# Second token group prepared in block 7, weight sums in two halves, and a block sum kept in SBUF

## The chip, the cores and the metric

The kernel runs on one core of one Trainium2 chip. TensorE (PE) does the matrix products, VectorE (DVE), ScalarE (ACT) and GpSimd (POOL) the element-wise work, and SyncE (SP) issues nearly all transfers; each of the five works through its own queue in order. The metric is the time of one execution in microseconds, as the median of several runs.

## The reference

Three networks follow each other. Attention over 4 x 8 heads of 576 positions, each query seeing up to 32 keys (dense for half of the heads, every fourth for the others); then a gated network; then eight experts, all of which see all 2304 tokens, weighted by a matrix P that is balanced in eight rounds.

```python
attn = softmax(masked(q @ k.T / 8)) @ v            # 2304 tokens x 512
x  = attn / rms(attn) * rms_g
x  = (silu(x @ w_gate) * (x @ w_val)) @ w_out      # 512 -> 1536 -> 512
P  = balance(exp(x @ w_gate2))                     # 2304 x 8
out = sum(P[:, e:e+1] * (relu(x @ w1[e]) @ w2[e])  # 512 -> 1024 -> 512
          for e in range(8))
```

## The kernel before

*Numbers in two parts.* Each operand of a product is split into a high part (a cast, ACT) and a low part (a subtraction, POOL or DVE), and three products high x high, high x low, low x high make one. So every operand costs a cast and a "low half".

*First network.* The tokens lie in eight blocks of 256 and 320. For each slice f of 128 hidden columns, `gemm_h` makes the gate (pg) and the value (pv); ACT's SiLU writes hf (L473), DVE multiplies (L474), ACT casts h (L475), POOL makes its low half (L476). Every four slices `gemm_out` adds up po, with ACT (L444) or DVE (L446) taking it out of PSUM into `partial`, which goes to x2d in DRAM (L448). Beside block i runs the attention of block i+1 (`att_tile`): the ssq of a tile gives its power on POOL (L292, an instruction of 128x2), DVE scales xs by it (L294), TensorE transposes it (L300). Beside it also run the `gate` of the experts, which fetches x2d slice by slice (sx, L582), casts it (g, L590) and makes its low half on POOL (L591), and `weight_sums`.

*Weight sums.* The second network multiplies blocks by a scheme with seven products (`STEPS`) in place of eight; for this it needs sums of weight blocks. `weight_sums` makes these for 16 chunks of both weights: 64 items, each loaded into one of three buffers (the unused parts of kbd and vbd, and conv), summed by four operations on POOL or DVE, and stored into `sums`. The four operations are ordered behind the newest hf product and h low half (`marks["late"]`).

*Token pieces.* The tokens are in three groups of 768. The sums and high and low parts of the first group's tokens are made at the end of block 7 (`tail`: `x_load`, `x_split`). Those of the other two are made by `x_prepare` during the second network, one group ahead: six pieces, each with four loads of 128x128 from x2d (xr), four subtractions on DVE, one cast on ACT (xh, L546) and one low half on DVE (xl, L549), and two stores to `xparts`. They take three tiles of the pool wx, from which the weights of the second network come too.

*Second network.* 48 units, 16 chunks for each of three groups. `gemm1(u)` makes seven products of 12 matmuls, `gemm2(u-1)` seven of 18, in turns. In the last step of `gemm1` the ReLU and four sums (`relu_with`, L998) give s1 to s4, which `summed` casts (L993) and halves (L994): s1 on DVE from PSUM, the others on POOL. In the first group the second weights are split from raw (L685, L686), and afterwards read back from DRAM.

*Order.* The functions above are generators, and `spread` advances them beside the matmuls' steps, so many steps of each to a block: 24 of `weight_sums`. A scheduler that simulates a timeline then sets the order of each queue from that; on the chip every queue runs in the order set.

## Time and profile before

| | us |
|---|---|
| median of three runs | 2108.41 (2107.94 to 2114.29) |
| profiled execution | 2112.69 |
| its span, first to last instruction | 2110.9 |
| TensorE busy in the span | 2023.5 |
| VectorE, ScalarE, GpSimd busy | 1440.8, 1097.3, 1167.6 |

In the rows of windows the busy times stand in the order PE, PEld (weight loads), DVE, ACT, POOL, then the granted clock, the busy share of the DMA engines and GB/s.

Attention and the first network fill the span up to about 640 us; the second network follows, its first group to about 1170 us. The granted clock in the windows is a share of TensorE's full 2.4 GHz: 0.50 is its lower level of 1.2 GHz. Idle time of an engine other than TensorE costs nothing by itself; it matters where TensorE waits behind it.

### The profile page before, as it was taken

The page shows a single profiled execution, that of the slowest core. Times are in us where ns is not written, and L with a number is a line of the kernel's source. Part 1 is how long each engine was busy: PE and PEld are TensorE (multiplying, and loading weights), DVE is VectorE, ACT ScalarE, POOL GpSimd, SP SyncE. Part 2 cuts the span into 40 slices and gives each one's busy share as a digit, 9 for nine tenths or more (in the row PEclk, how much of TensorE's full clock was granted, in tenths as well). Part 3 has the DMA queues.
Part 4 walks back from the last instruction along what each step waited for, and adds up shares of the span by engine and source line. Part 5 has one row for each costly group of instructions (what it writes and reads, how often), then busy time and mean ns, then how long its engine had stood idle before and what let it go on. Part 6 is the DMA issues. An engine that isn't in the chain of part 4 may idle for free.

```text
span 2110.9 us, 42653 instructions
## 1 busy us (share of the span) xinstructions
PE 2023.5 (96%) x16102; PEld 1976.6 (94%) x16102; DVE 1440.8 (68%) x3006; ACT 1097.3 (52%) x2408; POOL 1167.6 (55%) x1132
## 2 busy tenths in 40 slices
PE   5789999999998998999999999999999999999999
PEld 4688899899898998999999999999999999999999
DVE  7986544444435989888887676677766666667666
ACT  6564433333246575665656645555555645555553
POOL 3675555555555556766766545554554545544452
PEclk7899999999999999999999999999999999999999
DMA  8423676666647767788789756666668665566652
GB/s 269 146 74 104 236 254 223 239 234 213 215 138 267 253 218 257 267 287 293 255 284 362 250 190 199 230 230 222 215 214 293 235 200 183 187 210 200 198 178 85
DMA packets 210015, 464.69 MB, mean 220 GB/s; under 512 B 17168, under 2 KB 59920, under 8 KB 209808
## 3 DMA queue, kind: packets, MB, share of 16 engines
q1 hardware_dynamic: 202752, 442.97, 61.5%
q10 hardware_dynamic: 7056, 18.98, 2.8%
q8 instruction: 127, 2.08, 0.4%
q14 instruction: 80, 0.66, 0.1%
HBM read 349.16 MB, written 112.72 MB: 219 GB/s over the span
## 4 chain that ended last, share of the span: by engine, by line
PE 73%; DVE 9%; DMA 7%; POOL 4%; ACT 3%; issue 3%; SPq 1%; ACTq 0%; DVEq 0%; POOLq 0%
PE ya L1067 17%; PE pa L1014 16%; PE yb L1067 8%; PE pb L1014 8%; PE pv L461 5%; PE pg L461 5%; PE yc L1067 4%; PE po L435 4%; PE pc L1014 4%; DMA w0r<-in_w 2%; DMA sx<-x2d 1%; DMA sums<-vbd 1%; DMA w0s<-sums 1%; POOL w_s L686 1%; DVE h_a L986 1%
## 5 line engine op out<-in xcount | busy, mean ns | idle before, releaser
L686 POOL TENSOR_TENSOR w_s<-w0s,w_s 128x512 fp32r<-128x512 f32 x192 | 260.3, 1360 | 94.6 <-ACT w_s L685 94.5
L994 POOL TENSOR_TENSOR h_s<-p,h_s 128x384 fp32r<-128x384 f32 x96 | 103.4, 1098 | 354.7 <-ACT h_s L993 306.4
L686 POOL TENSOR_TENSOR w_a<-w0r,w_a 128x512 fp32r<-128x512 f32 x144 | 195.7, 1360 | 154.0 <-ACT w_a L685 153.4
L1103 DVE SCALAR_TENSOR_TENSOR acc<-ya,Pm,acc 128x256 f32<-128x256 f32 x510 | 220.9, 474 | 66.0 <-PE ya L1067 65.7
L1067 PE MATMUL ya<-w_t,h_s 128*128 128x256 f32 x1728 | 228.0, 283 | 1.6 <-ACT acc L1092 0.8
L1014 PE MATMUL pa<-x_t,w_s 128*128 128x384 f32 x1152 | 226.5, 338 | 2.5 <-ACT p L1026 2.5
L1067 PEld LDWEIGHTS ya<-w_t,h_s 128*128 128x128 f32 x1728 | 220.6, 190 | 2.6 <-ACT acc L1092 1.1
L1014 PEld LDWEIGHTS pa<-x_t,w_s 128*128 128x128 f32 x1152 | 199.9, 190 | 2.9 <-ACT p L1026 2.9
L461 PE MATMUL pv<-xn,w_v 128*128 128x320 f32 (+1 forms) x1152 | 185.6, 304 | 12.9 <-DVE w_v L380 3.6
L461 PE MATMUL pg<-xn,w_g 128*128 128x320 f32 (+1 forms) x1152 | 183.8, 303 | 3.9 <-DVE hf L474 2.5
L461 PEld LDWEIGHTS pv<-xn,w_v 128*128 128x128 f32 x1152 | 164.8, 193 | 18.9 <-DVE w_v L380 4.8
L435 PE MATMUL po<-h,w_o 128*128 128x320 f32 (+1 forms) x1152 | 175.6, 300 | 6.4 <-POOL w_o L378 1.6
L685 ACT CAST w_s<-w0s 128x512 fp32r<-128x512 f32 x192 | 120.2, 626 | 109.2 <-PE pb L1014 64.8
L1103 DVE SCALAR_TENSOR_TENSOR acc<-yb,Pm,acc 128x256 f32<-128x256 f32 x258 | 109.4, 475 | 93.0 <-PE yb L1067 92.8
L461 PEld LDWEIGHTS pg<-xn,w_g 128*128 128x128 f32 x1152 | 164.6, 193 | 8.1 <-DVE hf L474 3.3
L435 PEld LDWEIGHTS po<-h,w_o 128*128 128x128 f32 x1152 | 159.8, 189 | 11.0 <-DVE partial L446 2.6
L476 POOL TENSOR_TENSOR h<-hf,h 128x256 fp32r<-128x256 f32 (+1 forms) x96 | 82.2, 859 | 110.4 <-ACT h L475 110.1
L994 POOL TENSOR_TENSOR h_s<-r,h_s 128x384 fp32r<-128x384 f32 x96 | 98.9, 1053 | 53.0 <-ACT h_s L993 48.6
L1067 PE MATMUL yc<-w_b,h_a 128*128 128x256 f32 x864 | 124.1, 286 | 3.4 <-DVE acc L1096 1.6
L685 ACT CAST w_a<-w0r 128x512 fp32r<-128x512 f32 x144 | 89.5, 623 | 70.5 <-DMA w0r<-in_w 21.8
L1067 PE MATMUL yb<-w_t,h_s 128*128 128x256 f32 x864 | 121.8, 283 | 1.6 <-ACT h_s L993 1.0
L1067 PE MATMUL yb<-w_t,h_a 128*128 128x256 f32 x864 | 121.0, 282 | 1.8 <-DVE acc L1103 1.1
(258 smaller groups left out, 4749.0 us busy)
## 6 DMA issues: line engine op xcount, KB each, us to landing
w_t<-split SPq DMA_DIRECT2D x128, 512.0 KB, 4.3
w0r<-in_w SPq DMA_DIRECT2D x96, 512.0 KB, 6.4
w0s<-sums SPq DMA_DIRECT2D x96, 512.0 KB, 7.4
w_b<-split SPq DMA_DIRECT2D x96, 512.0 KB, 3.7
split<-w_t SPq DMA_DIRECT2D x64, 512.0 KB, 3.2
split<-w_b SPq DMA_DIRECT2D x48, 512.0 KB, 3.8
w1r<-in_w SPq DMA_DIRECT2D x32, 512.0 KB, 5.6
w1s<-sums SPq DMA_DIRECT2D x32, 512.0 KB, 7.6
```

Source lines behind the costliest of these rows:

```text
L435: nc.tensor.matmul(po[:, :n], lhsT=ow[f][:, a, dc * P : dc * P + P], rhs=hs[blk, f][:, bb, :n], start=k == 0, stop=k == 11,)
L461: nc.tensor.matmul(ps[:, :n], lhsT=w[kt, fg][:, a, fo * P : fo * P + P], rhs=xn[:, kt, bb, :n], start=k == 0, stop=k == 11,)
L476: late_g = nc.gpsimd.tensor_tensor(out=h[:, 1, :n], in0=hf, in1=h[:, 0, :n].bitcast(F32), op=ALU.subtract)
L685: nc.scalar.copy(v[:, :, 0, :], src)
L686: lo_eng.tensor_tensor(out=v[:, :, 1, :], in0=src, in1=v[:, :, 0, :].bitcast(F32), op=ALU.subtract)
L986: nc.vector.scalar_tensor_tensor(out=h[:, 1, :], in0=src, scalar=0.0, in1=h[:, 0, :].bitcast(F32), op0=ALU.max, op1=ALU.subtract)
L994: eng.tensor_tensor(out=h[:, 1, :], in0=src, in1=h[:, 0, :].bitcast(F32), op=ALU.subtract)
L1014: nc.tensor.matmul(ps, lhsT=w1s[u, a][:, kt, hl, q * P : q * P + P], rhs=xc[b, kt][:, xl, :TH], start=fresh and k == 0, stop=k == 5, skip_ ...
L1067: nc.tensor.matmul(ps, lhsT=hh[u, a, q][:, hl, jj * P : jj * P + P], rhs=w2s[u, b][:, q, wl, :], start=fresh and k == 0 and jj != 1, stop= ...
L1103: nc.vector.scalar_tensor_tensor(out=dst, in0=ps, scalar=scale, in1=dst, op0=ALU.mult, op1=ALU.add)
```

## The change

Three edits. The pieces of the second group (g = 1) are no longer made in the second network, but behind the weight sums, in the same three buffers (`ahead`); the third group's still are, by `x_prepare(2)` beside the second group. The four operations of a weight sum are given in two parts of two, each behind the newest marks, and `weight_sums` has three steps an item where it had two; `spread` now gets 39 steps a block. In `gemm1` the sum s1 is written over its operand u4 in SBUF and no longer over the PSUM bank; all low halves of s1 to s4 are on POOL, and they are made in the order s2, then s4 and s3, then s1.

```diff
+    def x_piece(g, k, c, raw, place):
+        b11, t3, t2, b21, t1, t4, b22 = (raw[:, P * j : P * j + P] for j in range(7))
+        for dst, i, j in ((b11, 0, 0), (t3, 0, 1), (b21, 1, 0), (b22, 1, 1)):
+            c0 = GT * g + TH * j + P * c
+            nc.sync.dma_start(dst, x2d[k + 2 * i, :, c0 : c0 + P])
+        yield
+        nc.vector.tensor_tensor(out=t1, in0=t3, in1=b11, op=ALU.subtract)
+        nc.vector.tensor_tensor(out=t3, in0=b22, in1=t3, op=ALU.subtract)
+        nc.vector.tensor_tensor(out=t2, in0=b22, in1=t1, op=ALU.subtract)
+        nc.vector.tensor_tensor(out=t4, in0=b21, in1=t2, op=ALU.subtract)
+        hi = place()
+        nc.scalar.copy(hi, raw)
+        yield
+        lo = raw.bitcast(F32R)
+        nc.vector.tensor_tensor(out=lo, in0=raw, in1=hi.bitcast(F32), op=ALU.subtract)
+        for n, t in enumerate((hi, lo)):
+            nc.sync.dma_start(
+                xparts[g - 1][:, k, :, n, P * c : P * c + P].rearrange("m p n -> p m n"),
+                t.bitcast(F32).rearrange("p (m n) -> p m n", m=7),
+            )
...
-            late.close()
-            nc.sync.dma_start(sums[w, ch][:, k, :], t.rearrange("p i n -> p (i n)"))
-            yield
-            load(i + 2)
-            yield
+            for part in range(2):
+                with ExitStack() as late:
+                    for m in marks["late"]:
+                        late.enter_context(tc.issue_after(m.ins))
+                    for out_, in0, in1, op in ops[2 * part : 2 * part + 2]:
+                        eng.tensor_tensor(out=out_, in0=in0, in1=in1, op=op)
+                if part:
+                    nc.sync.dma_start(sums[w, ch][:, k, :], t.rearrange("p i n -> p (i n)"))
+                    yield
+                    load(i + 2)
+                yield
+
+    def ahead():
+        yield from weight_sums()
+        places = [*set0.spare, conv[:, :1024]]
+        n = 0
+        for k in range(2):
+            for c in range(TH // P):
+                piece = x_piece(
+                    1, k, c, places[n % 3][:, : 7 * P], lambda n=n: places[(n + 1) % 3][:, : 7 * P].bitcast(F32R)
+                )
+                n += 2
+                for wait in (3, 2, 1):
+                    next(piece, None)
+                    for _ in range(wait):
+                        yield
...
-    sgen1 = weight_sums()
+    sgen1 = ahead()
     for i in range(2, 8):
-        sides = [(some(sgen1, 24), 24)]
+        sides = [(some(sgen1, 39), 39)]
...
-                    relu_with(r, c11, ps, ALU.subtract)
-                    relu_with(ps, c22, ps, ALU.add)
-                    relu_with(c11, c11, ps, ALU.subtract)
+                    relu_with(c22, c22, ps, ALU.add)
+                    relu_with(r, c11, ps, ALU.subtract)
+                    relu_with(c11, c11, c22, ALU.subtract)
                     relu_with(c21, c21, c11, ALU.add)
-                    t["s1", q] = ps
-        for names in ((("s1", "s1"), ("s2", "p1")), (("s3", "r"),), (("s4", "pq"),)):
+        for names in ((("s2", "p1"),), (("s4", "pq"), ("s3", "r")), (("s1", "u4"),)):
             for m, tag in names:
                 for q in range(2):
-                    summed(u, m, q, t[tag, q], nc.vector if m == "s1" else nc.gpsimd)
+                    summed(u, m, q, t[tag, q])
...
-        if u + NCH < n and units[u][1] == 3:
+        if u == NCH + 3:
             prep = x_prepare(units[u][0] + 1)
```

The queues move as follows. POOL in block 6, around the power of attention tile 18 (rstd_18), before; conv and kbd are weight sums, g1_3_1 and g1_3_2 the low halves of the gate's second and third slice:

```order
L654 TENSOR_TENSOR conv_91<-conv_91 128x256
L655 TENSOR_TENSOR conv_91<-conv_91 128x256
L591 TENSOR_TENSOR g1_3_1_6845<-sx_3_1_6813,g0_3_1_6844 128x384
L656 TENSOR_TENSOR conv_91<-conv_91 128x256
L591 TENSOR_TENSOR g1_3_2_6968<-sx_3_2_6949,g0_3_2_6967 128x384
L292 TENSOR_TENSOR rstd_18_6839<-rstd_18_6839,neghalf_79 128x2
L476 TENSOR_TENSOR h_6_5_6898<-hf_6_5_6899,h_6_5_6898 128x256
L658 TENSOR_TENSOR kbd_142<-kbd_142 128x256
L659 TENSOR_TENSOR kbd_142<-kbd_142 128x256
L660 TENSOR_TENSOR kbd_142<-kbd_142 128x256
L661 TENSOR_TENSOR kbd_142<-kbd_142 128x256
```

The same place after the change:

```order
L661 TENSOR_TENSOR conv_91<-conv_91 128x256
L661 TENSOR_TENSOR kbd_142<-kbd_142 128x256 x3
L592 TENSOR_TENSOR g1_3_1_6870<-sx_3_1_6842,g0_3_1_6869 128x384
L292 TENSOR_TENSOR rstd_18_6864<-rstd_18_6864,neghalf_79 128x2
L476 TENSOR_TENSOR h_6_5_6927<-hf_6_5_6928,h_6_5_6927 128x256
L661 TENSOR_TENSOR conv_91<-conv_91 128x256 x4
L592 TENSOR_TENSOR g1_3_2_6998<-sx_3_2_6974,g0_3_2_6997 128x384
L476 TENSOR_TENSOR h_6_6_7013<-hf_6_6_7014,h_6_6_7013 128x256
L661 TENSOR_TENSOR kbd_142<-kbd_142 128x256 x2
```

The power stood right behind the third slice's low half and stands now ahead of it and of the four conv operations.

ACT in block 7, before; po_7_0_0 to po_7_0_3 are the outputs that it copies out of PSUM:

```order
L475 CAST h_7_3_7532<-hf_7_3_7533 128x320
L473 ACTIVATE hf_7_4_7589<-pg_7_4_7552 128x320
L475 CAST h_7_4_7588<-hf_7_4_7589 128x320
L444 COPY partial_7_7600<-po_7_0_0_7601 128x320
L444 COPY partial_7_7600<-po_7_0_1_7621 128x320
L590 CAST g0_4_1_7665<-sx_4_1_7641 128x384
L473 ACTIVATE hf_7_5_7722<-pg_7_5_7689 128x320
L444 COPY partial_7_7600<-po_7_0_2_7645 128x320
L590 CAST g0_4_2_7753<-sx_4_2_7735 128x384
L473 ACTIVATE hf_7_6_7770<-pg_7_6_7739 128x320
L475 CAST h_7_5_7721<-hf_7_5_7722 128x320
L444 COPY partial_7_7600<-po_7_0_3_7669 128x320
```

The same place after, where the casts of 128x896 are those of the fourth, fifth and sixth token piece:

```order
L536 CAST vbd_143<-kbd_142 128x896
L475 CAST h_7_3_7565<-hf_7_3_7566 128x320
L473 ACTIVATE hf_7_4_7622<-pg_7_4_7580 128x320
L475 CAST h_7_4_7621<-hf_7_4_7622 128x320
L536 CAST kbd_142<-conv_91 128x896
L444 COPY partial_7_7636<-po_7_0_0_7637 128x320
L444 COPY partial_7_7636<-po_7_0_1_7661 128x320
L473 ACTIVATE hf_7_5_7767<-pg_7_5_7734 128x320
L591 CAST g0_4_1_7705<-sx_4_1_7681 128x384
L536 CAST conv_91<-vbd_143 128x896
L444 COPY partial_7_7636<-po_7_0_2_7685 128x320
L473 ACTIVATE hf_7_6_7822<-pg_7_6_7787 128x320
```

A cast of a piece now stands ahead of the first and of the third of these copies, and one ahead of h_7_3.

POOL in unit 34 of the second network, where the sums of unit 33 are halved, before:

```order
L994 TENSOR_TENSOR h_33_s2_0_21028<-p1_33_0_20643,h_33_s2_0_21028 128x384
L994 TENSOR_TENSOR h_33_s2_1_21031<-p1_33_1_20652,h_33_s2_1_21031 128x384
L686 TENSOR_TENSOR w1_35_a11_21101<-w0r_35_0_21036,w1_35_a11_21101 128x2x256
L686 TENSOR_TENSOR w1_35_a12_21129<-w0r_35_1_21038,w1_35_a12_21129 128x2x256
L994 TENSOR_TENSOR h_33_s3_0_21093<-r_33_0_20965,h_33_s3_0_21093 128x384
L994 TENSOR_TENSOR h_33_s3_1_21096<-r_33_1_20977,h_33_s3_1_21096 128x384
L994 TENSOR_TENSOR h_33_s4_0_21148<-pq_33_0_20773,h_33_s4_0_21148 128x384
L994 TENSOR_TENSOR h_33_s4_1_21151<-pq_33_1_20781,h_33_s4_1_21151 128x384
L686 TENSOR_TENSOR w1_35_s2_21156<-w0s_35_0_21040,w1_35_s2_21156 128x2x256
L686 TENSOR_TENSOR w1_35_s3_21182<-w0s_35_0_21040,w1_35_s3_21182 128x2x256
```

After:

```order
L1010 TENSOR_TENSOR h_33_s2_0_20998<-p1_33_0_20619,h_33_s2_0_20998 128x384
L1010 TENSOR_TENSOR h_33_s2_1_21001<-p1_33_1_20628,h_33_s2_1_21001 128x384
L702 TENSOR_TENSOR w1_35_a11_21077<-w0r_35_0_21006,w1_35_a11_21077 128x2x256
L702 TENSOR_TENSOR w1_35_a12_21105<-w0r_35_1_21008,w1_35_a12_21105 128x2x256
L1010 TENSOR_TENSOR h_33_s4_0_21063<-pq_33_0_20749,h_33_s4_0_21063 128x384
L1010 TENSOR_TENSOR h_33_s4_1_21066<-pq_33_1_20757,h_33_s4_1_21066 128x384
L1010 TENSOR_TENSOR h_33_s3_0_21069<-r_33_0_20941,h_33_s3_0_21069 128x384
L1010 TENSOR_TENSOR h_33_s3_1_21072<-r_33_1_20953,h_33_s3_1_21072 128x384
L1010 TENSOR_TENSOR h_33_s1_0_21124<-u4_33_0_20850,h_33_s1_0_21124 128x384
L1010 TENSOR_TENSOR h_33_s1_1_21127<-u4_33_1_20862,h_33_s1_1_21127 128x384
L702 TENSOR_TENSOR w1_35_s2_21132<-w0s_35_0_21010,w1_35_s2_21132 128x2x256
```

Where s3 and s4 followed the two weight halves, s4, s3 and s1 now do, so that s3 is third and fourth in that row and s1 comes behind it.

## Rows read from the trace of the kernel before

**Rows 1.** the page, busy time, share of the span, instructions of each engine
```profile
PE 2023.5 (96%) x16102; PEld 1976.6 (94%) x16102; DVE 1440.8 (68%) x3006; ACT 1097.3 (52%) x2408; POOL 1167.6 (55%) x1132
```

**Rows 2.** windows by stage: stretch, length, busy (instructions) of engines, clock, DMA
```profile
205.00:545.00 340.00, 326.45 (x3806) 310.29 (x3805) 156.60 (x319) 127.62 (x272) 181.71 (x231) 0.98 0.67 231
...
545.00:640.00 95.00, 93.40 (x725) 90.82 (x724) 37.64 (x75) 34.29 (x76) 50.05 (x56) 1.00 0.51 174
...
640.00:893.00 253.00, 237.07 (x1589) 230.87 (x1588) 207.97 (x410) 160.99 (x348) 156.12 (x123) 0.97 0.70 249
```

**Rows 3.** windows of 6, 2 and 30 units, cut at a unit's first matmul
```profile
893.59:1080.66 187.07, 182.54 (x1271) 179.27 (x1269) 161.22 (x299) 114.35 (x245) 128.94 (x98) 1.00 0.78 277
...
1080.66:1141.87 61.21, 59.90 (x412) 58.78 (x413) 47.81 (x95) 36.91 (x81) 41.88 (x33) 1.00 0.88 319
...
1171.58:2061.36 889.78, 889.78 (x6303) 889.74 (x6302) 604.30 (x1297) 474.94 (x1021) 452.75 (x390) 1.00 0.65 214
```

**Rows 4.** timeline: start, length, engine, line, instruction, idle time, releaser
```profile
395.25 0.66 PE L300 MATMUL psXT<-cst,xs 128*128 128x128 f32 x2 [3.71 <-DVE xs L294]
...
530.01 0.48 SPq L582 DMA_DIRECT2D sx<-x2d  x1
...
536.17 0.51 ACT L590 CAST g<-sx 128x384 fp32r<-128x384 f32 x1 [5.41 <-DMA sx<-x2d]
...
538.45 1.54 DVE L294 TENSOR_SCALAR xs<-xs,rstd 128x256 f32<-128x256 f32 x2 [4.84 <-POOL rstd L292]
...
539.40 0.66 PE L300 MATMUL psXT<-cst,xs 128*128 128x128 f32 x2 [4.05 <-DVE xs L294]
```

**Rows 5.** windows right behind the two gaps
```profile
395.00:400.00 5.00, 4.75 (x46) 3.78 (x47) 2.98 (x7) 1.40 (x3) 3.02 (x5) 0.50 0.68 194
...
539.00:543.00 4.00, 3.60 (x40) 2.63 (x41) 2.01 (x4) 1.00 (x2) 3.02 (x5) 0.50 0.52 169
```

**Rows 6.** window of DVE's instructions on the pieces (tile xr) alone
```profile
860.00:1170.00 310.00, 16.37 (x20) 1.00 0.80 289
```

**Rows 7.** DVE groups, 860 to 1170 us: count, busy us, mean ns, idle
```profile
L998 DVE SCALAR_TENSOR_TENSOR pq<-pq,p 128x384 f32<-128x384 f32 x20 | 13.7, 684 | 0.0
...
L998 DVE SCALAR_TENSOR_TENSOR p<-p,pa 128x384 f32<-128x384 f32 x20 | 10.8, 538 | 0.0
...
L994 DVE TENSOR_TENSOR h_s<-pa,h_s 128x384 fp32r<-128x384 f32 x20 | 10.8, 542 | 0.0
```

**Rows 8.** tiles xh and xl: ns shortest, median, longest; landing of stores
```profile
L546 ACT CAST xh<-xr x12: 932/944/995, 765.4 to 1539.9; 128x896 fp32r<-128x896 f32 x12
...
L549 DVE TENSOR_TENSOR xl<-xr,xh x12: 1074/1715/2186, 768.1 to 1549.8; 128x896 fp32r<-128x896 f32 x12
...
DMA to landing us min/median/max: 3.0/3.4/6.3
```

**Rows 9.** group on POOL, 860 to 1170 us
```profile
L994 POOL TENSOR_TENSOR h_s<-p,h_s 128x384 fp32r<-128x384 f32 x20 | 22.5, 1144 | 41.0 <-ACT h_s L993 20.9 <-DVE h_s L994 20.1
```

**Rows 10.** timeline of a unit of the third group
```profile
1628.67 2.01 POOL L994 TENSOR_TENSOR h_s<-pq,h_s 128x384 fp32r<-128x384 f32 x2
...
1630.62 1.31 POOL L686 TENSOR_TENSOR w_s<-w0s,w_s 128x512 fp32r<-128x512 f32 x1
...
1629.40 1.21 PE L1014 MATMUL pb<-x_t,w_s 128*128 128x384 f32 x6
...
1630.45 1.35 PE L1067 MATMUL yb<-w_t,h_s 128*128 128x256 f32 x10
```

**Rows 11.** timeline of block 7
```profile
571.76 0.46 ACT L475 CAST h<-hf 128x320 fp32r<-128x320 f32 x1 [1.86 <-DVE hf L474]
...
592.40 0.42 ACT L444 COPY partial<-po 128x320 f32<-128x320 f32 x1 [0.71 <-PE po L435]
...
599.35 0.42 ACT L444 COPY partial<-po 128x320 f32<-128x320 f32 x1 [2.56 <-PE po L435]
...
605.86 2.55 SPq L510 DMA_DIRECT2D xr<-x2d  x4
```

More of the change, by code (lines that the diff above doesn't have):

```diff
@@ L524, in x_prepare, with place @@
     def x_prepare(g):
+        def place(n, k, c):
+            t = wx.tile([P, 2, 512], F32R, tag="w", name=f"x{n}_{g}_{k}_{c}")
+            return t.rearrange("p s n -> p (s n)")[:, : 7 * P]
         for k in range(2):
             for c in range(TH // P):
-                raw = wx.tile([P, 2, 512], F32R, tag="w", name=f"xr_{g}_{k}_{c}").bitcast(F32)
-                raw = raw.rearrange("p s n -> p (s n)")[:, : 7 * P]
-                b11, t3, t2, b21, t1, t4, b22 = (raw[:, P * j : P * j + P] for j in range(7))
@@ L531, in x_prepare @@
-                for dst, i, j in ((b11, 0, 0), (t3, 0, 1), (b21, 1, 0), (b22, 1, 1)):
-                    c0 = GT * g + TH * j + P * c
-                    nc.sync.dma_start(dst, x2d[k + 2 * i, :, c0 : c0 + P])
-                for _ in range(6):
-                    yield
-                nc.vector.tensor_tensor(out=t1, in0=t3, in1=b11, op=ALU.subtract)
-                nc.vector.tensor_tensor(out=t3, in0=b22, in1=t3, op=ALU.subtract)
-                yield
-                nc.vector.tensor_tensor(out=t2, in0=b22, in1=t1, op=ALU.subtract)
@@ L551, in x_prepare @@
-                for n, t in enumerate((hi, lo)):
-                    nc.sync.dma_start(
-                        xparts[g - 1][:, k, :, n, P * c : P * c + P].rearrange("m p n -> p m n"),
-                        t.bitcast(F32).rearrange("p (m n) -> p m n", m=7),
-                    )
-                for _ in range(16):
-                    yield
+                piece = x_piece(g, k, c, place("r", k, c).bitcast(F32), lambda: place("h", k, c))
+                for wait in (6, 4, 17):
+                    next(piece, None)
+                    for _ in range(wait):
+                        yield
@@ L646, in weight_sums @@
             t = tiles.pop(i)
-            late = ExitStack()
-            for m in marks["late"]:
-                late.enter_context(tc.issue_after(m.ins))
             eng = (nc.gpsimd, nc.vector, nc.gpsimd)[i % 3]
```

32 lines of the change are left out of this document (9 added, 23 removed).

## The prediction

> **What bounds the kernel now.** I read the page first, then stretches of it, then TensorE's gaps. TensorE is busy 96% of the span [rows 1], so a gain can only come from the few per cent in which it waits or runs at the lower clock. The stretches say where they lie. The 30 units of the second network's second and third token groups take 889.78 us, 29.66 us each, and TensorE has no idle time in them: DVE at 20.1 us a unit and POOL at 15.1 us are hidden there, and nothing that the change does to them is worth time unless it makes TensorE wait. In the first group, six units with token pieces in them take 187.07 us, 31.18 each, with DVE busy 26.9 us of a unit; the two units behind them, where the pieces are finished, take 61.21 us, 30.6 each, with DVE at 23.9 [rows 3]. In the first network (205 to 545 us) TensorE is idle for 13.6 us, and from 640 to 893 us for 15.9 us; block 7 (545 to 640) loses 1.6 us, with DVE busy 40% and ACT 36% [rows 2].
>
> Two gaps of the first network stand out, at 395.25 (3.71 us) and 539.40 (4.05 us), both in front of an attention transpose [rows 4]. Read backwards, the second goes: the transpose waits for DVE's scaling (L294, idle 4.84 us), that for POOL's power (L292), and that stands in POOL's queue behind the low half of the gate's third token slice, which needs ACT's cast (536.17, idle 5.41 us), and that waits for the slice's DMA, issued at 530.01 behind the load of a block of weights. So a slice of 128 by 384 values for the gate, which nobody needs soon, stops the attention. Behind each gap the granted clock stands at 0.50, the 1.2 GHz level, for at least 5 and 4 us [rows 5]: half of that is lost as well, 4.5 us for both.
>
> **The change part by part.** The sum is made against the profiled execution: 2112.69 us, of which 1.79 us lie outside its span of 2110.9. It is 4.28 us (0.2%) above the median of 2108.41; I subtract the same sum from the median.
>
> *Weight sums in halves.* Operations and bytes stay; only the order moves, and each half may wait for the newest h product. In the queue rows of the change the power of tile 18 now stands ahead of the gate's third slice on POOL, with four weight-sum operations between; the same is so for tile 13, the gap at 395. Then neither transpose waits for the gate. I take out 7.76 us of gaps and 4.5 us of clock and leave 0.6 us each for what else is late there: 11 us gained. Bounds: 12.3 gained, or 0 if a similar queue forms elsewhere. Weight sums also run at 39 steps a block against 24, three to a sum in place of two: 13 sums a block against 12, which the idle half of POOL and DVE [rows 2] hides.
>
> *Pieces out of the first group.* Four pieces cost DVE 16.37 us between 860 and 1170 [rows 6], 4.1 each, so six take some 25 us from DVE; ACT loses six casts of 0.94 us [rows 8], SP 36 issues, and the ring of weight tiles three slots a piece. What a unit gains by this is measured: 31.18 against 30.6 us, 0.58 us, where DVE's load falls by 3 us. Pieces touch about 12 units: 7 us gained. Bounds: nothing, if the two piece-free units are faster for another reason; 18 us, if the stretch 640 to 893, which also holds pieces and idles most, answers more strongly.
>
> *The block sum in SBUF.* Per unit DVE loses two low halves of 0.54 us, and two of its subtractions now read two SBUF operands: 0.68 us as for pq<-pq,p against 0.54 us [rows 7]. That is 0.8 us less for DVE, which by the ratio above (0.58 per 3 us) is 0.15 us a unit over some 14 units: 2 us gained. POOL gets two low halves of 1.14 us more [rows 9], 2.3 us on 21.5 [rows 3], and is not full. The PSUM bank comes free two operations after the ReLU and not only after the low half; no row shows a wait on that worth a term. In the later 32 units all is hidden as long as POOL's row of s4, s3, s1 is in time. In before s4's two low halves end at 1630.68, and that place is now s3's [rows 10]. Before, s3 was read from 1630.45. The changed order lets the 12 matmuls of the next pb (1.05 us per six, by 1629.40 to 1630.45) go ahead of s3's first low half, so it is wanted near 1631.9: 1.2 us to spare. Taken as 0. Bounds for the whole edit: 11 us gained (0.8 us in 14 units), 28 us lost (rival 1).
>
> A row of the Trainium skill speaks against this edit: DVE with two SBUF inputs and a POOL operation that reads SBUF take a shared port as an exclusive lock, and the later one is blocked for the other's whole duration (SBUF — State Buffer, section "SBUF: two separate sides"). By that rule each new two-input subtraction could wait for a whole low half. The trace bears it out only in part: the two-input form takes 684 ns where the one with a PSUM operand takes 538, 0.15 us longer on average and not a whole POOL operation of 1.14 [rows 7, 9]. By the rule DVE's load would rise by 2 x 1.14 - 1.08 = 1.2 us a unit in place of falling, 3 us lost where I count 2 gained, and the forecast would be 2097; by the rows it stays.
>
> *Pieces in block 7.* Here they run as a chain: the cast of the next piece overwrites the tile from which the last low half is stored. One link is store to landing 3.4 us, cast 0.94, low half 1.1 to 2.2, issue 0.4 [rows 8]: about 6.0 us, with a low half near its shortest, since POOL has little to do here. The first cast follows h_7_0's (571.76 to 572.2), so the first low half ends near 574.5, the fifth cast near 574.5 + 3 x 6.0 + 4.7 = 597.2, the sixth near 603.2. In ACT's order they stand ahead of the first and third partial copies, which ran at 592.40 and 599.35 [rows 11]: 4.8 and 3.9 us late. TensorE has the next slice's 24 matmuls to do meanwhile, 3.1 us at the block's 93.4/725 us each [rows 2]; 1.7 and 0.8 us remain, with a little clock: 3 us lost. Bounds: 0 (ACT finds the cast ready) and 15 (rival 3). The x loads of the second network stand behind the last stores on SP, near 609 us in place of 605.86 [rows 11]; the work on them is wanted at 640, so they are covered. Two early reloads of group 1's first piece (two of 128x2x384) go ahead of the second weights' loads: 1 us lost, between 0 (they fit between transfers) and 4 (0.79 MB at the block's 174 GB/s [rows 2]).
>
> Sum: -11 - 7 - 2 + 3 + 1 = -16 us. The profile would show 2096.7, the median 2092.4: **2092 us**.
>
> **The rivals.** (1) *POOL's row is late in every unit, and the kernel is slower.* Six low halves now stand in one piece where four did. If they cost 1.3 us each, as POOL's weight halves in the same queue do [rows 10], and not 1.0, s3 is 1.2 us later, which uses up the 1.2 us; every further 0.6 us costs 0.6 x 46 units = 28 us: 2092 + 28 = 2120. It decides from the point where s3's second low half ends after 1631.9 in that unit. Against it: in that unit the pairs took 2.01 us [rows 10], and TensorE's order already puts other work there. The lock just cited would act in this direction, by 0.15 us an operation in the rows.
> (2) *The gate's wait comes back elsewhere.* The slice took 6 us from issue to cast [rows 4] behind a load of weights, such loads stay, and ACT and POOL still take them in order. What was behind them was an accident of order, and another may follow: first term 0, the others stay, 2103. For it: ACT's 5.41 us of idle time [rows 4] is there whoever stands behind it. Against: both powers are now clear of it.
> (3) *The chain in block 7 costs what was won.* If stores land in 6.3 us, the slowest seen [rows 8], a link takes 8.9 us; the fifth cast is some 13 us late and the sixth 15; with the cover of 3.1 us each and the clock 15 us are lost in place of 3: 2104. For it: in block 7 these stores share queue and engines with x2d and gate loads. Against: weight sums are finished by then.
>
> **How the numbers follow.** Forecast 0.55, rival (1) 0.10, (2) 0.20, (3) 0.15. 0.3% of 2108.4 is 6.3 us, about what this kernel's runs can tell from no change. Faster is below 2102.1: 0.53 from the forecast, 0.08 from (2), 0.05 from (3): 0.66. Within: 0.02 + 0.10 + 0.07 + 0.01 = 0.20. Slower: 0.09 from (1), 0.02 and 0.03 from the others: 0.14. The forecast's own range is 2082 to 2101 (its bounds taken together, most of them not at once). To hold 8 in 10 it must reach into (2) and (3): 2080 to 2111.
>
> **What would show it.** Right: no gap over 1.5 us in front of an attention transpose, and clock 1.00 where the two gaps were; the first group's middle units near 30.5 us, DVE near 23 us a unit; later units still 29.66; block 7 longer by 1 to 5 us with ACT idle ahead of the piece casts. Wrong: units of the later groups above 29.8 us with TensorE waiting for POOL's low halves; a gap of several us elsewhere with the gate's slice at its root; block 7 longer by more than 8 us; or middle units still at 31, which would mean that DVE's load was not what stretched them.

## The result, and the profile after

The changed kernel takes 2122.1 us (median of four runs, 2121.17 to 2123.47), the kernel before 2108.6 beside it: ratio 1.0058, 95% interval 1.004 to 1.0077. It is slower by some 13 us, where 2092 was predicted and the range ended at 2111. Its profiled execution has a span of 2121.2 us, against 2110.9.

Windows of both profiles cut at the same places of the program (a block of the first network by its first SiLU, a unit by its first matmul) say where it went. Columns as in [rows 2]. Before, blocks 2 to 6, block 7, units 0 to 7:

```profile
211.10:569.47 358.37, 344.82 (x3981) 329.14 (x3968) 165.69 (x342) 135.71 (x291) 192.32 (x246) 0.98 0.67 232
...
569.47:640.90 71.43, 69.83 (x476) 67.86 (x475) 27.11 (x48) 25.19 (x56) 38.77 (x42) 1.00 0.50 169
640.90:893.59 252.69, 236.76 (x1588) 230.56 (x1587) 208.56 (x411) 160.69 (x348) 156.52 (x123) 0.97 0.70 249
```

After, the same three, then the units of [rows 3]:

```profile
211.39:583.28 371.89, 348.03 (x3978) 334.15 (x3965) 166.82 (x350) 135.99 (x291) 202.21 (x261) 0.97 0.69 234
...
583.28:657.10 73.82, 70.56 (x479) 68.17 (x478) 36.38 (x70) 28.62 (x60) 27.16 (x25) 1.00 0.68 213
...
657.10:910.31 253.21, 236.78 (x1589) 230.00 (x1587) 205.29 (x383) 158.76 (x348) 174.04 (x139) 0.98 0.66 240
...
910.31:1090.96 180.65, 179.97 (x1261) 178.37 (x1261) 153.63 (x271) 112.05 (x241) 139.46 (x109) 1.00 0.73 262
1090.96:1150.76 59.80, 59.76 (x420) 59.35 (x420) 50.27 (x91) 37.45 (x81) 46.62 (x37) 1.00 0.90 319
...
1180.37:2072.14 891.77, 889.54 (x6302) 888.88 (x6301) 598.91 (x1242) 479.79 (x1023) 512.34 (x450) 1.00 0.67 213
```

Blocks 2 to 6 are 13.5 us longer, and there lies the loss: TensorE idles 23.9 us in place of 13.6 and is busy 3.2 us more, at a lower mean clock. Block 7 is 2.4 us longer. The first group gains: its six middle units 187.07 to 180.65 us, the next two 61.21 to 59.80. The 30 later units take 2.0 us more, all of it in two units of 31.0 and 31.2 us, in each of which TensorE waits 1.1 us for ACT (p) and not for POOL; the others stand at 29.63.

What TensorE waits for has changed. The two gaps of [rows 4] are gone (the same tiles' transposes now wait 1.06 us, at 398.56, and 0.04, at 547.92), and new ones stand elsewhere: 3.12 us at 251.51, 3.27 at 299.46, 3.71 at 323.26, 2.39 at 406.08, 2.90 at 574.65. The first three on TensorE (start, length, line, instruction, idle time and releaser):

```profile
251.51 0.41 PE L300 MATMUL psXT<-cst,xs 128*128 128x128 f32 x2 [3.12 <-DVE xs L294]
...
299.46 0.71 PE L461 MATMUL pv<-xn,w_v 128*128 128x320 f32 x3 [3.27 <-ACT hf L473]
...
323.26 1.11 PE L224 MATMUL psT<-cst,sc 128*128 128x128 f32 x4 [3.71 <-ACT sc L213]
```

DVE's timeline ahead of the first and the third of them:

```profile
247.88 1.80 DVE L661 TENSOR_TENSOR vbd<-vbd 128x256 f32<-128x256 f32 x4 [3.40 <-DMA vbd<-in_w]
249.60 0.15 DVE L291 SCALAR_TENSOR_TENSOR rstd<-psR,ssq 128x2 f32<-128x2 f32 x1
...
318.69 1.80 DVE L661 TENSOR_TENSOR vbd<-vbd 128x256 f32<-128x256 f32 x4 [8.20 <-DMA vbd<-in_w]
320.41 0.68 DVE L201 TENSOR_TENSOR sc<-psS,cst 128x512 f32<-128x512 f32 x1
```

DVE stands 3.4 and 8.2 us before a weight sum whose weights have not landed, and the attention's next operation is queued right behind it. The gap at 299.46 has the same root one queue further on. SyncE's timeline, and ACT's cast of the slice:

```profile
282.67 0.34 SPq L663 DMA_DIRECT2D sums<-kbd  x1
289.42 0.37 SPq L640 DMA_DIRECT2D kbd<-in_w  x1
289.88 1.93 SPq L448 DMA_DIRECT2D x2d<-partial  x2
291.86 0.43 SPq L663 DMA_DIRECT2D sums<-vbd  x1
294.06 0.32 SPq L583 DMA_DIRECT2D sx<-x2d  x1
...
297.15 0.51 ACT L591 CAST g<-sx 128x384 fp32r<-128x384 f32 x1 [8.31 <-DMA sx<-x2d]
```

SyncE stands at the load of kbd until the store out of kbd has landed (6.4 us); x2d is stored after that, the gate's slice is read after that, and ACT, with a SiLU behind the slice's cast, idles 8.31 us for it.

Followed back in this way, from releaser to releaser, the ten gaps of more than 0.7 us that TensorE has in these blocks (22.1 us) lead to the load of a weight sum in six (13.3 us), to a slice of the gate in three (7.7 us: at 299.46, 406.08 and 522.79) and to neither in one. Before, there were three such gaps (8.8 us), two of them, the 7.8 us of [rows 4], behind a slice and none behind a load.

All waits of sums for their loads in blocks 2 to 6 (us, times, longest), before:

```profile
POOL kbd L658 <- DMA kbd<-in_w: 4.2, 1, 4.2
POOL kbd L653 <- DMA kbd<-in_w: 0.8, 1, 0.8
```

and after, 73 us in 24 waits:

```profile
POOL kbd L661 <- DMA kbd<-in_w: 30.2, 10, 5.4
DVE vbd L661 <- DMA vbd<-in_w: 24.3, 7, 8.2
POOL conv L661 <- DMA conv<-in_w: 18.5, 7, 6.7
```

A buffer goes round: stored, loaded, left until its first operation, summed. The means over the 61 items behind the first three, from the issue and landing of each, are before 4.2 us store, 4.4 load, 5.1 left, 3.9 sum and 0.2 to the next store: 17.7 us before rounding, about three items at 12 a block. After: 4.4, 4.6, 2.8, 4.6 and 0.7, 17.0 us at 13 a block, whose blocks are longer. The pace took 0.7 us from the round, the halves 1.2 (a longer sum, a later store), slower transfers 0.4; what was left as cover fell from 5.1 us (5.4 in the expectations below) to 2.8, and 26 of 61 sums began within 0.3 us of their load's landing, where 3 of 61 had.

### The profile page after: what moved, and what is told of

Its sections match the earlier page's. It is cut to its first block, busy times and chain, and to the rows that moved or that the text cites. A ratio compares the mean times of both kernels' runs of the same rounds, so it can differ in the third digit from the quotient of the medians.

```text
span 2121.2 us, 42658 instructions
## 1 busy us (share of the span) xinstructions
PE 2027.7 (96%) x16102; PEld 1983.4 (94%) x16102; DVE 1435.9 (68%) x2910; ACT 1101.2 (52%) x2408; POOL 1264.4 (60%) x1228
## 4 chain that ended last, share of the span: by engine, by line
PE 68%; DMA 11%; DVE 9%; POOL 5%; issue 4%; ACT 2%; SPq 1%; DVEq 0%; ACTq 0%; POOLq 0%
PE ya L1082 16%; PE pa L1030 16%; PE yb L1082 8%; PE pb L1030 8%; PE yc L1082 4%; PE pc L1030 4%; PE pv L461 3%; PE pg L461 3%; PE po L435 3%; DMA sums<-kbd 2%; DMA sums<-vbd 1%; DMA vbd<-in_w 1%; DMA w0r<-in_w 1%; POOL w_s L702 1%; DMA sx<-x2d 1%
## 5 line engine op out<-in xcount | busy, mean ns | idle before, releaser
L1030 PE MATMUL pa<-x_t,w_s 128*128 128x384 f32 x1152 | 219.7, 338 | 5.6 <-ACT p L1042 5.2
L461 PE MATMUL pg<-xn,w_g 128*128 128x320 f32 (+1 forms) x1152 | 188.2, 307 | 3.0 <-DVE hf L474 2.5
L461 PEld LDWEIGHTS pv<-xn,w_v 128*128 128x128 f32 x1152 | 169.1, 198 | 22.0 <-ACT hf L473 6.9
L461 PEld LDWEIGHTS pg<-xn,w_g 128*128 128x128 f32 x1152 | 169.2, 197 | 6.4 <-DVE hf L474 3.0
L1010 POOL TENSOR_TENSOR h_s<-pq,h_s 128x384 fp32r<-128x384 f32 x96 | 96.9, 1031 | 62.4 <-ACT h_s L1009 62.4
L701 ACT CAST w_a<-w0r 128x512 fp32r<-128x512 f32 x144 | 89.6, 623 | 62.0 <-PE ya L1082 28.4
L1030 PE MATMUL pa<-x_b,w_a 128*128 128x384 f32 x576 | 114.9, 341 | 5.6 <-DVE r L1014 3.7
```

What stands on the lines that cost most here:

```text
L461: nc.tensor.matmul(ps[:, :n], lhsT=w[kt, fg][:, a, fo * P : fo * P + P], rhs=xn[:, kt, bb, :n], start=k == 0, stop=k == 11,)
L701: nc.scalar.copy(v[:, :, 0, :], src)
L1010: nc.gpsimd.tensor_tensor(out=h[:, 1, :], in0=src, in1=h[:, 0, :].bitcast(F32), op=ALU.subtract)
L1030: nc.tensor.matmul(ps, lhsT=w1s[u, a][:, kt, hl, q * P : q * P + P], rhs=xc[b, kt][:, xl, :TH], start=fresh and k == 0, stop=k == 5, skip_ ...
```

## The experiments

Theory A: in queues taken in order, sums wait for loads that land late, and attention and h stand behind them. Theory B: the gate's slices are at the root, as in the kernel before. Theory C: order or traffic itself. Ratios are to the kernel before on the same chip. "Waits" are those of sums for loads, 226 to 590 us; they and the lengths of blocks come from one profiled execution of each kernel. Five kernels with undivided sums at 12 items a block and late slices (before, e1, e5, e6, e8) took 355.6 to 358.4 us in blocks 2 to 6, so a difference of 3 us there says nothing. The second networks differ: all rows but before and e10 have the block sum; before, e10, e11 and e17 make no pieces of the second group in block 7, e12, e15 and e16 three, the others six. e5 to e9 are told in the text alone.

| | items a block | halves | slices ahead | waits, us (times) | blocks 2 to 6, us | ratio, interval |
|---|---|---|---|---|---|---|
| before | 12 | no | no | 5.0 (2) | 358.4 | 1 |
| after | 13 | yes | no | 73.0 (24) | 371.9 | 1.0058, 1.004 to 1.0077 |
| e1 | 12 | no | no | 10.7 (5) | 355.6 | 1.0011, 0.9999 to 1.0024 |
| e2 | 13 | no | no | 38.3 (21) | 371.5 | 1.0055, 1.0039 to 1.0071 |
| e3 | 12 | yes | no | 37.3 (13) | 361.2 | 1.0045, 1.0027 to 1.0063 |
| e4 | 13 | yes | no | 67.5 (24) | 372.0 | 1.0045, 1.0031 to 1.0059 |
| e10 | 12 | no | yes | 10.9 (7) | 347.0 | 0.9966, 0.9953 to 0.9979 |
| e11 | 12 | no | yes | 9.6 (5) | 347.2 | 0.9953, 0.9939 to 0.9968 |
| e12 | 12 | no | yes | 15.8 (7) | 348.5 | 0.9942, 0.9926 to 0.9958 |
| e13 | 13 | yes | yes | 96.0 (28) | 374.0 | 1.0078, 1.0063 to 1.0094 |
| e14, short loads | 13 | yes | no | 28.4 (13) | 350.4 | 0.9945, 0.993 to 0.996 |
| e15 | 12 | yes | yes | 40.3 (13) | 370.3 | 1.0033, 1.0016 to 1.0051 |
| e16 | 13 | no | yes | 48.5 (20) | 371.1 | 1.0034, 1.0021 to 1.0047 |
| e17 | 11 | no | yes | 27.3 (10) | 348.7 | 0.9953, 0.9935 to 0.9971 |

**e1 to e3: halves and pace taken apart**, in the changed kernel.

```diff
-            for part in range(2):          # e1, e2: one part, all four operations
+            for part in (1,):
...
-                    for out_, in0, in1, op in ops[2 * part : 2 * part + 2]:
+                    for out_, in0, in1, op in ops:
...
-        sides = [(some(sgen1, 39), 39)]
+        steps = 24 if i < 7 else 46        # e1; e2: 26 and 39; e3 (halves): 36 and 51
+        sides = [(some(sgen1, steps), steps)]
```

> The changed kernel with its weight sums undivided again and at the old pace (24 steps a block, 12 items, until block 6; in block 7 the 8 steps that are left and the six pieces). Theory A (late loads): a buffer of the weight sums is stored (4.2 us), loaded again (4.4 us) and summed (3.9 us) in turn, and three buffers at 12 items a block of some 72 us leave 5.4 us between landing and first operation; the change left 2.8 us, so that 24 loads were waited for on DVE and POOL with attention and h behind them. Then blocks 2 to 6 are as before here (the 13.8 us that they grew by are gone), block 7 keeps its 2 to 3 us, the second network its gain of 5.4 us: 2106, 0.1% under the kernel before. Theory B (the pieces and their traffic, or the s1 edit, lengthen the first network; the pace does not): it stays near 2120. Theory C (the accident of queue order): blocks 2 to 6 as before, with the gate's two gaps back, so the same as A here; the next two kernels tell A and C apart.

> The changed kernel with undivided sums at the changed kernel's pace (26 steps a block, 13 items). Theory A: the buffer's cycle is 16.6 us in place of 18 but the sum is no longer stretched, so 3.9 us are left between landing and first operation, between before (5.4) and after (2.8); fewer than 10 loads are waited for, and blocks 2 to 6 grow by 3 to 6 us: 2109 to 2113. Theory C (halves put operations of other work behind the gate and each other): with undivided sums nothing is cut, and blocks 2 to 6 come within 3 us of the kernel before: 2106. If the pace alone is the cause, all of the loss stays: 2119 or more.

> The changed kernel with sums in halves at the old pace (36 steps a block, 12 items; 51 in block 7). Theory A: the cycle is 18 us again but the sum is stretched (4.6 us and 0.7 to its store), 3.7 us are left between landing and first operation, and blocks 2 to 6 grow by 3 to 6 us: 2109 to 2113. If the halves with their marks are the cause alone, all of the loss stays: 2119 or more. If the forecast's own step was right and only the pace broke it, the two gaps at 395 and 539 are gone without others in their place, and blocks 2 to 6 are 8 to 11 us shorter than before: 2096 to 2098.

Without both, blocks 2 to 6 lose nothing (e1). The pace alone brings back the whole 13 us, more than theory A's 3 to 6; the halves alone cost 5.6 us against e1, in these blocks as in the medians (2120.7 against 2115.1; 2124.0 for the pace, whose block 7 has no sums left and is 6.1 us shorter than e1's). So each costs by itself, and the two together little more than the pace. In e1 the expected gain did not appear either: its second network is 8.9 us shorter than before, but block 7, with four sums left besides the six pieces, takes 83.2 us, 11.8 more.

**e4: each load of a sum given a step earlier**, with the store.

```diff
-                    yield
                     load(i + 2)
+                    yield
```

> The changed kernel with each load of the weight sums given one step earlier, together with the store, so five steps of 39 ahead of its sum in place of four. Theory A says that nothing is won: in the trace each load is already issued within 0.1 us of the landing of the store that frees its buffer, so SyncE waits there whoever gives it earlier; 2119 to 2126, and worse if SyncE's queue then holds back the gate's slices. The rival, that the loads are given too late in the order, expects the waits for loads (24 in the changed kernel) to fall by half and 5 to 8 us to come back: 2114 to 2117.

24 waits, 67.5 us, blocks 2 to 6 at 372.0: as theory A said, the load is held by the store that frees its buffer and not by its place in the order.

**e5, e6: the second network's two edits, each alone** in the kernel before (the diff of the change, its third part; and `ahead` with undivided sums, as in e1).

> The kernel before with the edit of the block sum alone (s1 over u4 in SBUF, all low halves on GpSimd, in the order s2, s4, s3, s1). The forecast's step: 2 us gained in the first group, nothing later, the first network as before: 2106 to 2107 on the chip of the first comparison, ratio 0.999. Rival 1 of the prediction (GpSimd's row late in each unit) would give 28 us more; the units of the changed kernel stand at 29.63, so it is not expected. If the second network's gain of 6 to 12 us came from this edit and not from the pieces, 2100, ratio 0.996.

> The kernel before with the second group's pieces made in block 7 alone (weight sums undivided at the old pace, 46 steps in block 7 for their last 8 and for the pieces; the block sum as before). If the pieces make the second network's gain, its first 17 units are 5 to 9 us shorter than before here too (the forecast's step said 7), and block 7, which took 83.2 us in the kernel of undivided sums at 12 items against 71.4 before, takes 81 to 85 again: the chain of piece, cast and store beside the second network's first loads and splits; ratio 1.001 to 1.004. If the block sum made the gain, the second network is as before within 3 us and the ratio is 1.005 or more.

e5: 0.9993 (0.9979 to 1.0007), second network 5.3 us shorter in the profile; e6: 1.0006 (0.9995 to 1.0018), 5.5 us shorter there, and block 7 at 82.3 us. In one profiled execution of each, either gives some 5 us and the two together 8.9 (e1), so they seem to overlap; the medians of e5 and e6 alone tell neither from no change. Nor are e5's 5.3 us mainly shorter waits: over the first 17 units, 6.0 us shorter, TensorE's idle time fell by 1.2 us and its busy time by 4.8, at a mean clock of 1.00 in place of 0.99.

**e7, e9: sums that need not wait for their loads** (in short form; `raw` is the block of weights, `nowhere` a place in DRAM).

```diff
-                nc.sync.dma_start(t, raw)
+                nc.sync.dma_start(t if i < 3 else nowhere[i % 3], raw)          # e7
+                nc.sync.dma_start(t if i < 3 else sums_of(items[i - 3]), raw)   # e9
```

> The changed kernel with the loads of the weight sums, from the fourth item on, sent to a place in DRAM that nobody reads, so that no sum waits for a load and no load for a store; it leaves out that the sums are those of the weights (they are made of what the buffers hold). Operations, steps, stores and the bytes read are those of the changed kernel. Theory A (late loads, in queues taken in order): the waits for loads on DVE and GpSimd are gone, and with them the gaps before the attention's transposes; blocks 2 to 6 fall from 371.9 us to 358 or less, the kernel before having 358.4: ratio 0.998 to 1.0. If the halves also take the powers out of the gate's way, as forecast, blocks 2 to 6 take 347 to 351: ratio 0.994 to 0.997. If the order itself or the traffic makes the gaps (theory C), blocks 2 to 6 stay at 367 or more: ratio 1.004 or more.

> The changed kernel with each load of the weight sums, from the fourth item on, sent over the sums that the item before in the same buffer has just stored: it stands at the same place of SyncE's queue, waits for the same store and moves the same bytes, but no sum waits for it (left out: the sums are made of stale data). In the run before, loads without any wait moved to the start of the kernel and took 25 us there, so that its total says little; its blocks 2 to 6 took 337.6 us, with TensorE waiting 1.2 us, at 164 GB/s. Theory A (DVE and GpSimd wait in order for loads that land late): blocks 2 to 6 take 340 to 352 us in place of 371.9 (before: 358.4), at some 230 GB/s, and the ratio is 0.990 to 0.997. Theory C (traffic, or SyncE's queue, which holds back the gate's slices): they stay at 362 or more, ratio 1.001 or more.

e7: 1.0002 (0.9989 to 1.0016). Blocks 2 to 6 took 337.6 us with 1.6 us of gaps, but the loads, bound to nothing, were all issued early: 302 GB/s up to 100 us, where the changed kernel has 213, and block 2 began 25 us later. So waits and traffic had both gone. e9 kept the loads in their place, and blocks 2 to 6 took 379.0 us: 1.0061 (1.0042 to 1.0079). The sums had moved forward in the queues and now waited for the stores:

```profile
DVE vbd L665 <- DMA sums<-vbd: 21.1, 7, 5.7
POOL kbd L665 <- DMA sums<-kbd: 16.9, 6, 5.4
POOL conv L665 <- DMA sums<-conv: 12.4, 5, 6.6
```

My expectation that nothing would be waited for was wrong; neither run tells A from C. e9 shows only that waits for stores, in 18 places, go with as long blocks as waits for loads; of its gaps over 0.7 us (26.0 us), 8.4 us lead back to such a store and 17.6 to a slice of the gate.

**e8, e10, e11, e12: the gate's wait taken away.** e8 only gives the slice's load two steps earlier; e10 needs one tile fewer for a slice.

```diff
-            hi, lo = (stg.tile(...) for s in range(2))
+            hi = stg.tile(...)
+            if kt < 3:
+                ahead_of = load(kt + 1)
             nc.scalar.copy(hi, st)
+            lo = st.bitcast(F32R)
             nc.gpsimd.tensor_tensor(out=lo, in0=st, in1=hi.bitcast(F32), op=ALU.subtract)
+            st = ahead_of
...
-            if kt < 3:
-                st = load(kt + 1)
```

> The kernel before with each of the gate's later token slices loaded three steps ahead of its cast in place of one (2.1 us a step). The gate's wait was what stopped the attention at 395 and 539 us (7.8 us of gaps and some 4.5 us at the lower clock). If the slice's lead is what was short, ACT's waits for slices of about 5 us are gone and with them both gaps: blocks 2 to 6 take 347 to 352 us in place of 358.4, ratio 0.995 to 0.997. If SyncE's queue holds the slices back whoever gives them earlier (it stands at the weight sums' loads until their buffers' stores land), nothing changes: ratio 0.999 to 1.001. If the earlier load only makes SyncE wait for GpSimd's low half and holds back weight loads behind it, 1.002 or more.

> The kernel before with the gate's low half written over its token slice (two tiles of the ring a slice in place of three), so that the next slice is loaded four steps ahead of its cast and does not wait for GpSimd's low half; in the run before the earlier load alone moved nothing, because the slice still waited for that buffer (issued at 386.51 behind the low half that began at 385.28). If the gate's wait is what stops the attention at 395 and 539, ACT's waits of 5 us for slices and both gaps go: blocks 2 to 6 take 346 to 351 us in place of 358.4, ratio 0.994 to 0.997. If something else is late behind it, 355 to 358: ratio 0.998 to 1.001.

> The edit of the block sum with the gate's slices loaded ahead, in the kernel before. The gains lie in different stages, so they add up: second network 5 us shorter (as with the block sum alone), blocks 2 to 6 shorter by what the gate alone gives (7 to 12 us): ratio 0.992 to 0.996. If they do not add up because a later start finds its weights late, 0.997 or more.

> The same two edits, and three of the second group's six pieces made in block 7 (28 steps there: 8 for the last weight sums, which are undivided at the old pace, and the pieces), the other three in the second network. Six pieces with the last sums made block 7 11.7 us longer and the first group 4 us shorter than the block sum alone; if the chain of pieces grows with their number, three cost 2 to 5 us and bring 2: ratio 0 to 0.2% above the kernel with the two edits alone. If only the end of the chain beside the second network's first loads costs, three pieces cost nothing, and it is 0.1% below.

e8 moved nothing (0.9991, 0.9978 to 1.0004; both gaps stay, 3.86 and 3.71 us): the slice waited for the buffer that the low half before it was still reading. e10 took both gaps to 1.0 and 1.1 us:

```profile
214.07:561.07 347.00, 338.82 (x3981) 325.26 (x3968) 169.36 (x342) 136.69 (x290) 194.54 (x246) 1.00 0.70 239
```

Clock 1.00, the 2.4 GHz level, all through, and 11.4 us gained in these blocks (5.4 of idle time, 6.0 of busy time): the size that the prediction gave to the two gaps, 11, was right. With the block sum (e11) and three pieces in block 7 (e12) it is the fastest kernel of the study, 2098.8 us against 2110.3, 0.58% under the kernel before; the intervals of e11 and e12 overlap.

**e13, e14: which transfer.** e13 is e10's edit in the changed kernel; e14 cuts the loads (in short form; `src` is the block of weights).

```diff
+                part = 512 if i < 3 else 128
-                nc.sync.dma_start(t, src)
+                nc.sync.dma_start(t[:, :, :part], src[:, :, :part])    # e14
```

> The changed kernel with the gate's slices loaded ahead (low half over the slice), nothing else. This edit alone took 11.3 us out of blocks 2 to 6 of the kernel before. Theory B (the changed kernel's new gaps have the gate's slices at their root): blocks 2 to 6 fall from 371.9 us to 350 or less, ratio 0.995. Theory A (late loads of the weight sums): the gaps behind ACT's waits for slices go (about 6 us with their clock), those behind DVE's and GpSimd's waits for loads stay: 362 to 368, ratio 1.001 to 1.004.

> The changed kernel with the loads of the weight sums cut to a quarter of their bytes from the fourth item on (128 of 512 columns; left out: the rest of the sums is made of stale data). Steps, operations, stores and nearly all of the queues' order are those of the changed kernel. Theory A: loads land 1 to 2 us sooner, the waits for loads (73 us in 24) fall by more than half, and blocks 2 to 6 fall from 371.9 to 352 to 362, ratio 0.997 to 1.002. Theory B (the gate's slices): little changes there, 366 or more, ratio 1.003 or more.

With the gate out of the way the changed kernel is no faster (e13); theory B falls, and A's own figure, 362 to 368, was too low. In e13, 20.6 of the 26.1 us in gaps over 0.7 us lead back to a sum's load and 3.8 to a slice. With shorter loads (2.9 us in place of 4.6) the loss is gone, and a gain of 8.0 us against the kernel before appears; 1.5 of the 8.2 us in such gaps lead to a load. Windows of blocks 2 to 6, and the waits of sums, of e14:

```profile
211.16:561.52 350.36, 339.35 (x3978) 326.30 (x3965) 166.67 (x350) 136.07 (x290) 203.08 (x261) 1.00 0.53 180
```

```profile
POOL kbd L663 <- DMA kbd<-in_w: 10.8, 6, 3.2
POOL conv L663 <- DMA conv<-in_w: 9.8, 4, 4.4
DVE vbd L663 <- DMA vbd<-in_w: 7.8, 3, 2.7
```

Operations and steps are the changed kernel's. The traffic is less (180 against 234 GB/s) and stores land sooner too (3.6 us), so this shows that the loss comes with how long the loads take, not that traffic has no part in making them long.

**e15, e16: halves and pace, each in e12.** `for part in range(2)` with 36 steps (32 in block 7); and 26 steps (20 in block 7).

> The kernel with the block sum, the gate's slices loaded ahead and three pieces in block 7, with the weight sums in halves at the old pace (36 steps, 12 items a block; 32 in block 7). If halves cost by stretching the sum and storing it later (4.7 us against 3.9 in the runs so far), blocks 2 to 6 take 3 to 8 us more than the 348.5 of that kernel with undivided sums: ratio 0.996 to 0.998. If they only cost together with the gate's wait, the same within 2 us: 0.994.

> The same kernel with undivided sums at 13 items a block (26 steps; 20 in block 7, all of them for the pieces). If the pace costs by taking 1.5 us from a buffer's cycle (24 sums waited for their load in the run with 13 items, 6 with 12), blocks 2 to 6 take 6 to 12 us more than 348.5, and block 7 is 2 to 4 us shorter, since no weight sums are left for it: ratio 0.996 to 0.999. If the pace only costs together with the gate's wait, 0.993.

Each costs 22 us in blocks 2 to 6, far more than theory A's 3 to 12, and 0.9% of the time. Windows of e15 and e16:

```profile
210.53:580.87 370.34, 346.81 (x3978) 332.63 (x3966) 168.54 (x342) 135.84 (x291) 193.71 (x248) 0.97 0.66 225
```

```profile
211.48:582.57 371.09, 346.14 (x3987) 331.92 (x3975) 174.23 (x350) 135.85 (x291) 203.56 (x260) 0.98 0.69 235
```

TensorE idles 23.5 and 25.0 us again, and the clock is back at 0.97 and 0.98. Of the gaps over 0.7 us, at least 14 of 19.7 us in e15 and 18.4 of 23.6 us in e16 lead back to a sum's load, where e12 has 2.6 of 5.6. e15 moves nearly the same bytes as e12, at 225 GB/s in place of 237 since its blocks are longer, so more traffic is not what makes its gaps. Nor does the mean of the cover tell: 4.7 us in e15, 4.3 in e12, but 14 of e15's 61 sums began within 0.3 us of their load's landing and 8 of e12's. e12's window:

```profile
212.04:560.56 348.52, 340.26 (x3981) 326.70 (x3969) 168.34 (x342) 136.62 (x290) 193.74 (x246) 1.00 0.69 237
```

**e17: a slower pace.**

```diff
-        sides = [(some(sgen1, 24), 24)]
+        steps = 22 if i < 7 else 24
+        sides = [(some(sgen1, steps), steps)]
```

> The kernel with the block sum and the gate's slices loaded ahead (all pieces in the second network, sums undivided) at 11 items a block in blocks 2 to 6 (22 steps in place of 24; the rest in block 7, 24 steps there). At 12 items five sums waited 9.6 us for their loads, and blocks 2 to 6 took 347.2 us. If what is lost is the waits for loads, a cycle that is 1.6 us longer takes most of the rest: 343 to 346 us there, and 0 to 3 us more in block 7: ratio 0.994 to 0.996, against 0.9953. If the pace cost by itself (operations and traffic beside the matmuls), 5 sums less would give 341 or less. If order decides more than either, anything up to 355.

No gain: 27.3 us of waits in ten, blocks 2 to 6 at 348.7, 1.5 us more than e11. Slack on the mean is not all. Over the table, up to 28 us of waits cost little, and 37 us or more cost 5.6 to 27 against the kernel with the same gate; the loss does not follow the waits in proportion (37 us cost 5.6 in e3, 38 us cost 15.9 in e2). That it depends on what stands behind each wait fits the chains above, but was not tried by itself.

## Why the prediction was wrong

*Weight sums in halves, -11 us.* This step failed: +13.5 us in blocks 2 to 6, and nothing there in e1, which keeps the other two edits. The order did what was read from it: the powers are clear of the slices, and both gaps went. But "operations and bytes stay; only the order moves" left out the round of the buffers, and "13 sums a block against 12, which the idle half of POOL and DVE hides" weighed the pace by the engines' idle time, where the transfers between sums had no room. Its lower bound, 0, was wrong for the same reason. The row was there to be read: in the kernel before, SyncE waited 111.7 us at the sums' loads for stores to land (us, times, longest), and two sums already waited for their loads.

```profile
SPq L639 <- DMA sums<-vbd: 51.8, 20, 5.9
...
SPq L639 <- DMA sums<-conv: 38.4, 19, 4.1
...
SPq L639 <- DMA sums<-kbd: 21.5, 18, 2.7
```

e2, e3, e15 and e16 show that either part of the edit, the halves or the pace, costs by itself; e14 that 8.0 us of the forecast's 11 are there when loads land sooner.

*Pieces -7, block sum -2.* The sum, 9, came out in e1 (8.9) but not in the changed kernel's profile (5.9), and the split was wrong: 5.5 and 5.3 us alone. So that the sum fits is in part luck, and the price of DVE's load, 0.58 us per 3, is not shown: e5's gain was not mainly one of waits. A middle unit came to 30.1 us, near the 30.5 named as the sign, though DVE's load fell from 26.9 to 25.6 us and not to 23: it was worth more than 0.58 us per 3, or was not all. On DVE the edit of the block sum saved less than reckoned. DVE's groups from 660 to 2100 us, before:

```profile
L998 DVE SCALAR_TENSOR_TENSOR pq<-pq,p 128x384 f32<-128x384 f32 x96 | 59.4, 621 | 0.2 <-ACT pq L1032 0.2
...
L998 DVE SCALAR_TENSOR_TENSOR p<-p,pa 128x384 f32<-128x384 f32 x96 | 51.8, 541 | 0.0
```

and after:

```profile
L1014 DVE SCALAR_TENSOR_TENSOR pq<-pq,p 128x384 f32<-128x384 f32 x94 | 81.2, 881 | 0.8
L1014 DVE SCALAR_TENSOR_TENSOR p<-p,u 128x384 f32<-128x384 f32 x94 | 59.9, 637 | 0.0
```

The new two-input form costs 0.10 us more than the one it replaces, where I counted 0.14; but pq, two-input before and after, costs 0.26 more. For two of each that is 0.7 us a unit, against 1.1 saved on two low halves: 0.4 us less where I counted 0.8. In the 30 later units DVE's busy time fell by only 0.2 us a unit (604.3 to 598.9 us), since h_a<-u, which did not change, rose from 892 to 1007 ns as well. By the estimate from the rule of the Trainium skill on the shared port (SBUF — State Buffer, section "SBUF: two separate sides") it would have been 1.2 more. The rows lie between: pq is longer by a quarter of one of GpSimd's low halves on the mean; that it is longer because of them was not tried.

*Pieces in block 7, +3, and reloads, +1.* +2.4 us measured in block 7, with ACT idle ahead of the casts as described (the second and the sixth of six); no run tells the reloads apart:

```profile
591.65 0.94 ACT L536 CAST kbd<-conv 128x896 fp32r<-128x896 f32 x1 [1.54 <-DMA xparts<-kbd]
...
615.11 0.94 ACT L536 CAST conv<-vbd 128x896 fp32r<-128x896 f32 x1 [3.13 <-DMA xparts<-conv]
```

The last cast came 31.8 us after the block's first SiLU, as reckoned (603.2 is 33.7 after it). The stores of the pieces landed in 3.1 us on the mean (longest 3.7), near the 3.4 assumed. e1 and e6 show what the low price rested on: all weight sums finished before. With four left, these stores take 5.3 and 5.0 us on the mean (longest 8.4 and 8.9), the chain runs into the second network's first loads, and block 7 is 11 us longer: that is rival 3, where what was named against it, finished weight sums, does not hold. In rival 3's own sum the fifth and sixth casts come 16.4 and 18.4 us late; its 13 and 15 are what the cover of 3.1 leaves.

*The rivals.* (1) did not occur: 28 of the 30 later units are at 29.63 or near it, and the two others wait for ACT. (2) was nearest, a wait that comes back elsewhere, and its sign was there, a gap of 3.27 us with a slice at its root. But it was put at a net of nothing and on the slice alone; with 13.3 us of gaps behind the sums' own loads against 7.7 behind slices it came back larger, and e13, without most of the waits for slices, is no faster.

## What to carry to other kernels

When work is paced faster or cut in pieces, add up the round of its buffers (store, landing, load, landing, operation) and compare it with the items' distance; an engine's idle time says nothing about that. The mean of what is left is only a first look, as e15 and e17 show: count the items that find none. In queues taken in order, an operation that waits for a transfer costs what stands behind it, so look at what is queued there before giving it an earlier place. And the wait for the slice went when the buffer that held the transfer back was freed (e10), not when the load was given earlier (e8) or the order turned round it (the change).

## What the runs showed of the hardware

A load of a quarter of the bytes (128 KB in place of 512) landed in 2.9 us (e14), the whole in 4.6: 1.7 us went with 384 KB, so some 2.3 of the 4.6 us, an estimate by a straight line through the two, do not go with the bytes. It is a rough one, since less traffic ran beside the shorter loads (180 GB/s against 234). The Trainium skill (DMA: Bandwidth & Descriptors, section "Anatomy of one DMA — SWDGE (gpsimd) path") has about 2.0 us of that kind, for transfers issued from GpSimd, where these are issued from SyncE.

TensorE's clock does not follow the length of a gap alone. Windows of the changed kernel right behind the gaps of 3.27, 3.71, 2.39 and 2.90 us:

```profile
299.50:303.00 3.50, 3.50 (x25) 3.50 (x26) 2.06 (x4) 2.27 (x7) 2.31 (x3) 1.00 1.03 347
323.30:328.00 4.70, 4.70 (x18) 4.46 (x19) 1.49 (x4) 2.45 (x4) 0.00 (x0) 0.50 0.84 263
406.10:409.00 2.90, 2.67 (x13) 2.46 (x14) 2.37 (x5) 1.51 (x4) 2.01 (x3) 0.65 0.94 297
574.70:577.00 2.30, 2.30 (x11) 2.30 (x12) 1.52 (x7) 0.74 (x3) 0.26 (x1) 0.50 0.27 78
```

Behind the first it stands at 2.4 GHz, behind the second and the last at 1.2; behind the third, the shortest, the mean of 0.65 says that it fell within the window.
